# Re-ordering the start, the second batch's loads and scores, the folds and the tail of a fused attention-plus-FFN kernel

## The chip, the cores and the metric

The kernel runs on one core of a Trainium2 chip. The metric is the device time of one execution in microseconds (us), as the median of several. A run counts as slow when it is over 1.5% above the fastest of the same kernel; the texts below compare fast runs unless they say otherwise. "Same" means within 2%.

TensorE does the matmuls (PE in the profile), VectorE is DVE, ScalarE is ACT, GpSimd is POOL and SyncE is SP. Idle time of TensorE is what costs, since it is busy nearly throughout. "Before" is the kernel before the change, "the change" the changed kernel.

## The reference, cut to what matters

```python
# q, k, v: (4, 5824, 256) float32; tau = 1
qn = q / (norm(q, axis=1) + 1e-6);  kn = k / (norm(k, axis=1) + 1e-6)
s  = kn.transpose(0, 2, 1) @ qn / tau          # 256 x 256 for each batch
a  = softmax(s, axis=-1)
x  = (v @ a).reshape(4 * 5824, 256)
out = ((x @ w1) * (x @ w2)) @ w3 @ w_out       # d_ff = 1024
```

The kernel folds the attention matrix into the weights: for each batch, `Wf = a @ (w1, w2)`, so that `v` is multiplied straight by `Wf`; and `W = w3 @ w_out` once. A batch is 11 chunks of 512 tokens and a short one, each with 8 units: two TensorE products a and b of `v` with a part of `Wf`, and their elementwise product. Of the 192 tokens of a short chunk, the 64 beyond 128 are the left-over rows; those of two batches are handled together. The fold needs the whole scores of its batch, and those need all of its q and k.

## The kernel before

All loads come from GpSimd, which casts float32 to bf16 on the way; SyncE issues most transposes of v and most output stores. A batch's q and k come in six pieces each; q has five buffers, k six, v three.

```python
IN_BUFS = {"q": 5, "k": 6, "v": 3}
...
def load_part(nm, n, pi, lo, hi):
    nc.gpsimd.dma_start(
        out=pieces[nm, n, pi][:, lo:hi, :], in_=qk_main[nm, n][0][:, pi * PIECE + lo : pi * PIECE + hi, :]
    )
...
def transpose_piece(n, pi):                     # v is wanted transposed
    ...
        nc.sync.dma_start_transpose(vT[:, pi * PIECE : (pi + 1) * PIECE, :, :], t[:, :, :])
```

Work other than the units is kept in an agenda. Its times are not times of the chip but a sum of the estimated TensorE costs of what has been emitted, the `clock`; I call its unit a clock-us. A unit adds 0.87, a deferred fold 0.43. What is due is emitted between units.

```python
def run_due(upto=None):
    lim = clock[0] if upto is None else upto
    while agenda and agenda[0][0] <= lim:
        _, _, cost, fn = agenda.pop(0)
        clock[0] += cost
        fn()
...
def make_agenda(b):
    clock[0] = 0.0
    if b == 0:
        for i in range(2):
            at(1.5 + 0.6 * i, 0.43, soft0[5 + i])          # two folds left over
        ...
        moves = [("v", 0, 3, 29.0), ("qk", 1, 0, 38.0), ("qk", 1, 1, 43.0), ("v", 0, 4, 50.0), ("qk", 1, 2, 58.0)]
        moves += [("qk", 1, 3, 63.0), ("v", 0, 5, 70.0), ("qk", 1, 4, 81.0), ("qk", 1, 5, 87.0)]
        ...
        t0, t1 = 57.0, 115.5                               # scores of the second batch
```

GpSimd takes the moves in order. Ahead of each, it copies one element of the newest product (a gate: not before TensorE has got there), and, if the move before was a v, one element of that v's **transposed** tile. I call that a hold: the next load isn't issued until the transpose has landed.

```python
for nm, m, pi, t in moves:
    if before is not None:
        at(t, 0.0, lambda w=before: hold(vTs[w[0]][...]))  # nc.gpsimd.tensor_copy(gate_t, src)
    at(t, 0.0, gate)
    if nm == "qk":
        at(t, 0.0, lambda m=m, pi=pi: load_qk(m, pi))
        before = None
    else:
        at(t, 0.0, lambda m=m, pi=pi: load_piece("v", m, pi))
        at(t + 4.0, 0.0, lambda m=m, pi=pi: transpose_piece(m, pi))
        before = (m, pi)
for i, (cst, fn) in enumerate(score_units(n)):
    at(t0 + (t1 - t0) * i / len(units), cst, fn)
```

Of the kernel before, what the change touches and what calls it, by code (L numbers as in the profile page):

```python
# [10 lines left out]
AF = mybir.ActivationFunctionType  # L11
ALU = mybir.AluOpType
F32 = DT.float32
BF16 = DT.bfloat16

P = 128
PIECE = 8
LAG = 2
IN_BUFS = {"q": 5, "k": 6, "v": 3}
MM_COL = 1.0 / 2400.0  # L20
MM_FIX = 0.0025
# [3 lines left out]
def kernel(  # L25
# [213 lines left out]
    def soft_units(n):  # L239
# [102 lines left out]
        def fold_mm(i, c2, tag="ab", on_act=None):  # L342
            h, rest = divmod(i, 4)
            w, c1 = divmod(rest, 2)
            if c2 == 0:
                st["fold", i] = psum.tile(
                    [P, 512], F32, tag=tag, name=f"fold_{n}_{i}", bufs={"ab": 4, "out": 3}[tag]
                )
            nc.tensor.matmul(  # L349
                st["fold", i], lhsT=st["e"][:, c2, c1 * P : (c1 + 1) * P], rhs=w12[:, c2, w, h * 512 : (h + 1) * 512],  # L350
                start=(c2 == 0), stop=(c2 == CT - 1),
            )
            if c2 == CT - 1:
                dst = Wf[n][:, c1, w, h * 512 : (h + 1) * 512]
                if on_act if on_act is not None else i % 2 == 0:
                    nc.scalar.activation(out=dst, in_=st["fold", i], func=AF.Copy, scale=st["rs"][:, c1 : c1 + 1])  # L356
                else:
                    nc.vector.tensor_scalar_mul(dst, st["fold", i], st["rs"][:, c1 : c1 + 1])

        def fold(i, tag="ab", on_act=None):  # L360
            fold_mm(i, 0, tag)
            fold_mm(i, 1, tag, i % 2 == 0 if on_act is None else on_act)

        def first_folds():
            sum_mm(0)
            fold_mm(0, 0)
            fold_mm(1, 0)
            sum_mm(1)
            fold_mm(0, 1)
            fold_mm(1, 1)  # L370
            fold(2)
            transpose_half_on_pe(0, 0, 0, False)
            fold(3, on_act=True)
            fold(4, "out", on_act=False)
            fold(5, "out")

        if n == 0:
            return [k_first, k_row, q_first, scaled_first, first_folds] + [lambda i=i: fold(i) for i in range(6, 8)]
# [7 lines left out]
            + [(0.2, 15.5, sums)]  # L386
            + [(0.43, 16.5 + 0.85 * i, lambda i=i: fold(i)) for i in range(8)]
# [75 lines left out]
    def emit_out(b, c, j, ab):  # L463
# [13 lines left out]
        for s, lhsT in enumerate(lhs):  # L477
            h, o = (s, 0) if small else divmod(s, 2)
            nc.tensor.matmul(  # L479
                tl[h][:, o, :], lhsT=lhsT, rhs=W_sb[:, j, :],  # L480
                start=(j == 0 and o == 0), stop=(j == FT - 1 and (small or o == 1)),
                skip_group_check=True,
            )
        clock[0] += len(lhs) * (D * MM_COL + MM_FIX)
        if j == FT - 1:
            o = work.tile([P, 4, D], F32, tag="o_sb", name=f"osb_{b}_{c}", bufs=3)
            rows = out[b * N : b * N + NT * P, :].rearrange("(p i) c -> p i c", i=NT)
            if small:
                nc.scalar.copy(o[:, 0, :], tl[0][:, 0, :])
                other = nc.scalar if b == B - 1 else nc.sync  # L490
                other.dma_start(out=rows[:, NT - 1, :], in_=o[:, 0, :])
                if b % 2 == 1:
                    o2 = work.tile([P, D], F32, tag="kr", name=f"oleft_{b}", bufs=1)
                    nc.vector.tensor_copy(o2, tl[1][:, 0, :])
                    for k, eng in enumerate((nc.sync, other)):
                        m = b - 1 + k
                        eng.dma_start(out=out[m * N + NT * P : (m + 1) * N, :], in_=o2[k * LEFT : (k + 1) * LEFT, :])
# [4 lines left out]
            del out_tiles[b, c]  # L502
# [9 lines left out]
    busy(14)  # L512
    load_piece("k", 0, 0, (half,))
    load_piece("q", 0, 0, (half,))
# [14 lines left out]
    nc.vector.tensor_tensor_scan(idx, ones_pp, ones_pp, 0.0, ALU.mult, ALU.add)  # L529
    turned = psum.tile([P, 512], F32, tag="ab", name="turned", bufs=4)  # L530
# [31 lines left out]
    for h in range(2):  # L562
        hs = slice(h * F // 2, (h + 1) * F // 2)
        nc.gpsimd.dma_start(out=w12[:, :, 0, hs], in_=w1r[:, :, hs])
        nc.gpsimd.dma_start(out=w12[:, :, 1, hs], in_=w2r[:, :, hs])
        if h == 0:
            new_piece("v", 0, 0)
        load_part("v", 0, 0, h * half, (h + 1) * half)
# [20 lines left out]
    busy(4)  # L589
# [23 lines left out]
    def make_agenda(b):  # L613
# [3 lines left out]
        if b == 0:  # L617
            for i in range(2):
                at(1.5 + 0.6 * i, 0.43, soft0[5 + i])
# [8 lines left out]
            moves = [("v", 0, 3, 29.0), ("qk", 1, 0, 38.0), ("qk", 1, 1, 43.0), ("v", 0, 4, 50.0), ("qk", 1, 2, 58.0)]  # L628
            moves += [("qk", 1, 3, 63.0), ("v", 0, 5, 70.0), ("qk", 1, 4, 81.0), ("qk", 1, 5, 87.0)]
            moves += [("v", 1, 0, 96.0), ("v", 1, 1, 106.0), ("v", 1, 2, 116.0), ("qk", 2, 0, 126.0)]  # L630
            t0, t1 = 57.0, 115.5
        else:
# [4 lines left out]
            t0, t1 = 16.0, 104.0  # L637
# [24 lines left out]
    for b in range(B):  # L662
        make_agenda(b)
        for c in range(NCH):
            for j in range(FT):
# [3 lines left out]
                while w_ready[0] and len(pend) > LAG and npop < 2:  # L669
                    emit_out(*pend.pop(0))  # L670
                    npop += 1
                    run_due()
        run_due(1e9)
    while pend:
        emit_out(*pend.pop(0))
# [35 lines left out]
```

## Time and profile before

| | before |
|---|---|
| median of 3 runs | 573.14 us |
| span of the profiled execution | 571.7 us |
| TensorE busy | 559.4 us |
| first unit starts | 40.7 us |
| last matmul ends | about 567.9 us |

Read the busy row first. TensorE is busy for 98% of the span. Timeline columns are the start in us, the duration, the engine, the line, the operation, and in brackets the idle time before it with what ended it.

```profile
139.19 0.60 PE L188 MATMUL G<-k,q 128*128 128x256 bf16 x4
```

### The profile page before, as it was taken

The page shows a single profiled execution, that of the slowest core. Times are in us where ns is not written, and L with a number is a line of the kernel's source. Part 1 is how long each engine was busy: PE and PEld are TensorE (multiplying, and loading weights), DVE is VectorE, ACT ScalarE, POOL GpSimd, SP SyncE. Part 2 cuts the span into 40 slices and gives each one's busy share as a digit, 9 for nine tenths or more (in the row PEclk, how much of TensorE's full clock was granted, in tenths as well). Part 3 has the DMA queues.
Part 4 walks back from the last instruction along what each step waited for, and adds up shares of the span by engine and source line. Part 5 has one row for each costly group of instructions (what it writes and reads, how often), then busy time and mean ns, then how long its engine had stood idle before and what let it go on. Part 6 is the DMA issues. An engine that isn't in the chain of part 4 may idle for free.

```text
span 571.7 us, 10102 instructions
## 1 busy us (share of the span) xinstructions
PE 559.4 (98%) x3750; PEld 354.5 (62%) x3750; DVE 377.4 (66%) x612; ACT 337.7 (59%) x624; POOL 83.3 (15%) x164
## 2 busy tenths in 40 slices
PE   7789999999999999999999999999999999999997
PEld 4655576776666666666666666666665666666665
DVE  1047744788977567887776667778876656565564
ACT  0046644777856567776766567767766554454453
POOL 5250020303030111121030012031120000000000
PEclk9999999999999999999999999999999999999999
DMA  8999959869685697495661595665640325221011
GB/s 163 211 187 208 184 104 240 170 149 242 140 183 118 123 204 150 94 192 121 145 144 72 99 215 123 140 136 126 175 110 38 85 73 148 63 63 75 38 72 58
DMA packets 74560, 76.93 MB, mean 135 GB/s; under 512 B 54160, under 2 KB 58256, under 8 KB 74512
## 3 DMA queue, kind: packets, MB, share of 16 engines
q0 software_dynamic: 15504, 39.46, 39.3%
q1 hardware_dynamic: 58784, 36.64, 22.2%
q8 instruction: 29, 0.48, 0.3%
q10 hardware_dynamic: 224, 0.20, 0.1%
q14 instruction: 19, 0.16, 0.1%
HBM read 78.91 MB, written 23.86 MB: 180 GB/s over the span
## 4 chain that ended last, share of the span: by engine, by line
PE 92%; DMA 5%; DVE 1%; ACT 1%; POOL 1%; issue 0%; ACTq 0%; POOLq 0%
PE o L479 28%; PE a L438 27%; PE b L438 27%; PE G L188 5%; DMA k<-in_k_dram 5%; PE fold L349 2%; PE w L596 1%; ACT as L444 0%; ACT kr L279 0%; POOL k L109 0%; POOL q L109 0%; DVE abs L453 0%; PE sqk L221 0%; DVE vT L136 0%; DVE abs L455 0%
## 5 line engine op out<-in xcount | busy, mean ns | idle before, releaser
L453 DVE TENSOR_TENSOR abs<-as,b 128x512 bf16<-128x512 bf16 x336 | 230.5, 687 | 141.4 <-ACT as L444 130.3
L444 ACT CAST as<-a 128x512 bf16<-128x512 f32 (+1 forms) x384 | 216.1, 563 | 176.9 <-DVE abs L453 90.2
L438 PEld LDWEIGHTS <-Wf 128*128 128x128 bf16 x1536 | 149.2, 98 | 102.0 <-issue 1.9
L479 PE MATMUL o<-W_sb,abs 128*128 128x256 bf16 x1376 | 209.6, 273 | 0.1
L438 PE MATMUL a<-vT,Wf 128*128 128x512 bf16 x704 | 209.4, 379 | 0.2
L438 PE MATMUL b<-vT,Wf 128*128 128x512 bf16 x704 | 209.3, 379 | 0.0
L479 PEld LDWEIGHTS <-abs 128*128 128x128 bf16 x1376 | 134.5, 98 | 81.6 <-DVE abs L455 0.3
L197 DVE TENSOR_TENSOR acc<-acc,sq 128x1024 f32<-128x1024 f32 x66 | 80.4, 1219 | 0.4 <-ACT sq L185 0.3
L188 PE MATMUL G<-k,q 128*128 128x256 bf16 x276 | 49.9, 273 | 0.0
L185 ACT ACTIVATE sq<-q 128x512 f32<-128x512 bf16 x66 | 41.8, 634 | 0.0
L185 ACT ACTIVATE sq<-k 128x512 f32<-128x512 bf16 x66 | 41.6, 630 | 0.0
L426 POOL COPY gate_t<-abs 1x1 bf16<-1x1 bf16 x39 | 13.9, 355 | 167.7 <-DVE abs L453 167.0
L500 DVE COPY osb<-o 128x512 f32<-128x512 f32 x44 | 30.1, 685 | 0.7 <-PE o L479 0.7
L430 POOL COPY gate_t<-vT 1x1 bf16<-1x1 bf16 x17 | 4.4, 258 | 169.3 <-DMA vT<-v 134.0
L188 PEld LDWEIGHTS <-q 128*128 128x128 bf16 x276 | 27.0, 98 | 3.1
L499 ACT COPY osb<-o 128x512 f32<-128x512 f32 x44 | 25.8, 586 | 3.8 <-PE o L479 1.8
L279 ACT ACTIVATE kr<-row 128x256 f32<-128x256 f32 x1 | 0.4, 385 | 31.6 <-PE row L267 31.6
L109 POOL DMA_DIRECT2D q<-in_q_dram x29 | 15.7, 541 | 13.2 <-DMA k<-in_k_dram 6.0
L349 PE MATMUL fold<-w,e 128*128 128x512 bf16 x64 | 17.0, 380 | 0.5 <-DVE vT L136 0.4
L356 ACT ACTIVATE Wf<-fold,rs 128x512 bf16<-128x512 f32 x16 | 10.9, 688 | 8.1 <-PE fold L349 6.4
L244 DVE TENSOR_TENSOR dk<-sqk,ident 128x256 f32<-128x256 f32 x1 | 0.4, 425 | 21.3 <-PE sqk L221 21.3
L109 POOL DMA_DIRECT2D k<-in_k_dram x25 | 13.8, 551 | 3.7 <-DMA k<-in_k_dram 1.9
(89 smaller groups left out, 240.4 us busy)
## 6 DMA issues: line engine op xcount, KB each, us to landing
out_dram<-osb SPq DMA_DIRECT2D x44, 512.0 KB, 3.1
k<-in_k_dram POOLq DMA_DIRECT2D x19, 512.0 KB, 8.5
v<-in_v_dram POOLq DMA_DIRECT2D x19, 512.0 KB, 5.2
q<-in_q_dram POOLq DMA_DIRECT2D x18, 512.0 KB, 6.6
w_wout<-in_moe_w_dram POOLq DMA_DIRECT2D x1, 2048.0 KB, 23.6
k<-in_k_dram POOLq DMA_DIRECT2D x4, 320.0 KB, 9.9
v<-in_v_dram POOLq DMA_DIRECT2D x4, 320.0 KB, 5.4
q<-in_q_dram POOLq DMA_DIRECT2D x4, 256.0 KB, 12.0
```

Of the source, the lines that this page charges most:

```text
L109: nc.gpsimd.dma_start(out=pieces[nm, n, pi][:, lo:hi, :], in_=qk_main[nm, n][0][:, pi * PIECE + lo : pi * PIECE + hi, :])
L185: nc.scalar.activation(out=dst[:, :, part, :], in_=src[:, o : o + 2, :], func=AF.Square)
L188: nc.tensor.matmul(G[:, ct, :], lhsT=qt[:, i, ct * P : (ct + 1) * P], rhs=kt[:, i, :], start=(pr == 0 and part == 0 and ct == 0), stop=(pr ...
L197: nc.vector.tensor_add(accs[n], accs[n], sqs[0])
L349: nc.tensor.matmul(st["fold", i], lhsT=st["e"][:, c2, c1 * P : (c1 + 1) * P], rhs=w12[:, c2, w, h * 512 : (h + 1) * 512], start=(c2 == 0), ...
L426: nc.gpsimd.tensor_copy(gate_t, last_ab[0][:1, :1])
L438: nc.tensor.matmul(t[:, :n], lhsT=Wf[b][:, ct, w, j * P : (j + 1) * P], rhs=rhs_of(b, c, ct), start=(ct == 0), stop=(ct == CT - 1),)
L444: nc.scalar.copy(a_sb[:, :n], tiles[0][:, :n])
L453: nc.vector.tensor_mul(ab, a_sb, tiles[1])
L479: nc.tensor.matmul(tl[h][:, o, :], lhsT=lhsT, rhs=W_sb[:, j, :], start=(j == 0 and o == 0), stop=(j == FT - 1 and (small or o == 1)), skip ...
L499: nc.scalar.copy(o[:, 0:2, :], tl[0])
L500: nc.vector.tensor_copy(o[:, 2:4, :], tl[1])
```

## The change

The intent is to fill idle time of TensorE at the start, at the three batch changes and at the end. (1) The first halves of the first q and k come as float32 from SyncE and are cast on chip. (2) The first batch's folds are done by quarters, so that the first unit can start after one quarter; more folds are left for later. (3) In the first batch, the loads of the second batch's q and k go ahead of late v pieces, and the scores run from 46 to 104 clock-us in place of 57 to 115.5. (4) In later batches scores end sooner, softmax and folds are spaced further out, and every second fold uses the scores' one-buffer bank G of PSUM (TensorE's output memory) in place of the four buffers "ab" of the units. (5) In the last short chunk the outputs are held back by five units, and at the end the left-over rows go first. The cut leaves out the new functions, the order of v's first load among the weights, and one transpose of v that moves ahead of the first fold.

```diff
+LAG_END = 5
...
-            + [(0.2, 15.5, sums)]
-            + [(0.43, 16.5 + 0.85 * i, lambda i=i: fold(i)) for i in range(8)]
+            + [(0.2, 16.5, sums)]
+            + [(0.43, 17.8 + 0.9 * i, lambda i=i: fold(i, "G" if i % 2 else "ab")) for i in range(8)]
...
-    busy(14)
-    load_piece("k", 0, 0, (half,))
-    load_piece("q", 0, 0, (half,))
+    busy(10)
+    raw = {}
+    for nm in "kq":
+        new_piece(nm, 0, 0)
+        raw[nm] = work.tile([P, half, C], F32, tag="o_sb", name=f"raw_{nm}", bufs=3)
+        nc.sync.dma_start(out=raw[nm], in_=qk_main[nm, 0][0][:, :half, :])
+        load_part(nm, 0, 0, half, PIECE)
...
+    nc.vector.tensor_copy(pieces["k", 0, 0][:, :half, :], raw["k"])
+    nc.scalar.copy(pieces["q", 0, 0][:, :half, :], raw["q"])
...
-    for h in range(2):
-        hs = slice(h * F // 2, (h + 1) * F // 2)
...
+    for f0, f1 in ((0, 256), (256, 512), (512, F)):
+        nc.gpsimd.dma_start(out=w12[:, :, 0, f0:f1], in_=w1r[:, :, f0:f1])
+        nc.gpsimd.dma_start(out=w12[:, :, 1, f0:f1], in_=w2r[:, :, f0:f1])
...
-            for i in range(2):
-                at(1.5 + 0.6 * i, 0.43, soft0[5 + i])
+            at(0.5, 0.87, soft0[5])
+            for i in range(4):
+                at(2.3 + 0.6 * i, 0.43, soft0[6 + i])
...
-            moves = [("v", 0, 3, 29.0), ("qk", 1, 0, 38.0), ("qk", 1, 1, 43.0), ("v", 0, 4, 50.0), ("qk", 1, 2, 58.0)]
-            moves += [("qk", 1, 3, 63.0), ("v", 0, 5, 70.0), ("qk", 1, 4, 81.0), ("qk", 1, 5, 87.0)]
-            moves += [("v", 1, 0, 96.0), ("v", 1, 1, 106.0), ("v", 1, 2, 116.0), ("qk", 2, 0, 126.0)]
-            t0, t1 = 57.0, 115.5
+            moves = [("qk", 1, 0, 29.0), ("v", 0, 3, 30.0), ("qk", 1, 1, 43.0), ("qk", 1, 2, 47.0), ("v", 0, 4, 53.0)]
+            moves += [("qk", 1, 3, 62.0), ("qk", 1, 4, 66.0), ("v", 0, 5, 72.0), ("qk", 1, 5, 81.0)]
+            moves += [("v", 1, 0, 94.0), ("v", 1, 1, 104.0), ("v", 1, 2, 114.0), ("qk", 2, 0, 126.0)]
+            t0, t1 = 46.0, 104.0
...
-            t0, t1 = 16.0, 104.0
+            t0, t1 = 16.0, 99.0
...
-                while w_ready[0] and len(pend) > LAG and npop < 2:
+                lag = LAG_END if b == B - 1 and c == NCH - 1 else LAG
+                while w_ready[0] and len(pend) > lag and npop < 2:
...
-    while pend:
-        emit_out(*pend.pop(0))
+    for only in (1, 0):
+        for p in pend:
+            emit_out(*p, only=only)
```

More of the change, by code (lines that the diff above doesn't have):

```diff
@@ L340, in sums, with fold_mm @@
             sum_mm(1)
-        def fold_mm(i, c2, tag="ab", on_act=None):
-            h, rest = divmod(i, 4)
-            w, c1 = divmod(rest, 2)
+        def fold_mm(key, c2, tag="ab", on_act=True):
+            w, c1, lo, hi = key
             if c2 == 0:
-                st["fold", i] = psum.tile(
-                    [P, 512], F32, tag=tag, name=f"fold_{n}_{i}", bufs={"ab": 4, "out": 3}[tag]
+                st[key] = psum.tile(
+                    [P, 512], F32, tag=tag, name=f"fold_{n}_{w}_{c1}_{lo}", bufs={"ab": 4, "out": 3, "G": 1}[tag]
                 )
+            m = st[key][:, : hi - lo]
             nc.tensor.matmul(
-                st["fold", i], lhsT=st["e"][:, c2, c1 * P : (c1 + 1) * P], rhs=w12[:, c2, w, h * 512 : (h + 1) * 512],
+                m, lhsT=st["e"][:, c2, c1 * P : (c1 + 1) * P], rhs=w12[:, c2, w, lo:hi],
                 start=(c2 == 0), stop=(c2 == CT - 1),
@@ L353, in fold_mm @@
             if c2 == CT - 1:
-                dst = Wf[n][:, c1, w, h * 512 : (h + 1) * 512]
-                if on_act if on_act is not None else i % 2 == 0:
-                    nc.scalar.activation(out=dst, in_=st["fold", i], func=AF.Copy, scale=st["rs"][:, c1 : c1 + 1])
-                else:
-                    nc.vector.tensor_scalar_mul(dst, st["fold", i], st["rs"][:, c1 : c1 + 1])
-        def fold(i, tag="ab", on_act=None):
-            fold_mm(i, 0, tag)
-            fold_mm(i, 1, tag, i % 2 == 0 if on_act is None else on_act)
+                dst = Wf[n][:, c1, w, lo:hi]
@@ new lines, in fold_mm, with fold, quarter_mm @@
+                if on_act:
+                    nc.scalar.activation(out=dst, in_=m, func=AF.Copy, scale=st["rs"][:, c1 : c1 + 1])
+                else:
+                    nc.vector.tensor_scalar_mul(dst, m, st["rs"][:, c1 : c1 + 1])
+        def fold(i, tag="ab"):
+            h, rest = divmod(i, 4)
+            w, c1 = divmod(rest, 2)
+            for c2 in range(CT):
+                fold_mm((w, c1, h * 512, (h + 1) * 512), c2, tag, i % 2 == 0)
+        def quarter_mm(lo, c1, c2):
+            if c2 == 0:
+                tag = "ab" if lo == 0 else "out"
+                st[lo, c1] = psum.tile(
+                    [P, 2, 256], F32, tag=tag, name=f"quarter_{lo}_{c1}", bufs={"ab": 4, "out": 3}[tag]
+                )
+            m = st[lo, c1]
+            for w in range(2):
+                nc.tensor.matmul(
+                    m[:, w, :], lhsT=st["e"][:, c2, c1 * P : (c1 + 1) * P], rhs=w12[:, c2, w, lo : lo + 256],
+                    start=(c2 == 0 and w == 0), stop=(c2 == CT - 1 and w == 1), skip_group_check=True,
+                )
+            if c2 == CT - 1:
+                for o in (0, P) if lo == 0 else (slice(0, 256),):
+                    cols = slice(o, o + P) if lo == 0 else o
+                    dst, src = Wf[n][:, c1, :, lo : lo + 256][:, :, cols], m[:, :, cols]
+                    if c1 == 0:
+                        nc.scalar.activation(out=dst, in_=src, func=AF.Copy, scale=st["rs"][:, c1 : c1 + 1])
+                    else:
+                        nc.vector.tensor_scalar_mul(dst, src, st["rs"][:, c1 : c1 + 1])
@@ L364, in first_folds @@
         def first_folds():
             sum_mm(0)
-            fold_mm(0, 0)
-            fold_mm(1, 0)
+            for c1 in range(CT):
+                quarter_mm(0, c1, 0)
             sum_mm(1)
-            fold_mm(0, 1)
-            fold_mm(1, 1)
-            fold(2)
-            transpose_half_on_pe(0, 0, 0, False)
-            fold(3, on_act=True)
-            fold(4, "out", on_act=False)
-            fold(5, "out")
+            for c1 in range(CT):
+                quarter_mm(0, c1, 1)
@@ L377, in soft_units, with second_quarter @@
+        def second_quarter():
+            for c1 in range(CT):
+                for c2 in range(CT):
+                    quarter_mm(256, c1, c2)
         if n == 0:
-            return [k_first, k_row, q_first, scaled_first, first_folds] + [lambda i=i: fold(i) for i in range(6, 8)]
+            return [k_first, k_row, q_first, scaled_first, first_folds, second_quarter] + [lambda i=i: fold(i) for i in range(4, 8)]
         return (
@@ L461, in emit_ab, with emit_out @@
         clock[0] += 4 * (n * MM_COL + MM_FIX)
-    def emit_out(b, c, j, ab):
+    def emit_out(b, c, j, ab, only=None):
         small = c == NCH - 1
@@ L477, in emit_out @@
         for s, lhsT in enumerate(lhs):
+            if only is not None and s != only:
+                continue
             h, o = (s, 0) if small else divmod(s, 2)
@@ L483, in emit_out @@
             )
-        clock[0] += len(lhs) * (D * MM_COL + MM_FIX)
+        clock[0] += (len(lhs) if only is None else 1) * (D * MM_COL + MM_FIX)
         if j == FT - 1:
@@ L488, in emit_out @@
             if small:
-                nc.scalar.copy(o[:, 0, :], tl[0][:, 0, :])
                 other = nc.scalar if b == B - 1 else nc.sync
-                other.dma_start(out=rows[:, NT - 1, :], in_=o[:, 0, :])
-                if b % 2 == 1:
+                if only != 1:
+                    nc.scalar.copy(o[:, 0, :], tl[0][:, 0, :])
+                    other.dma_start(out=rows[:, NT - 1, :], in_=o[:, 0, :])
+                if b % 2 == 1 and only != 0:
                     o2 = work.tile([P, D], F32, tag="kr", name=f"oleft_{b}", bufs=1)
@@ L501, in emit_out @@
                 nc.sync.dma_start(out=rows[:, 4 * c : 4 * c + 4, :], in_=o)
-            del out_tiles[b, c]
+            if only is None:
+                del out_tiles[b, c]
     NDEF = 4
@@ L561 @@
     load_piece("q", 0, 5, (1, 3, 4))
-    for h in range(2):
-        hs = slice(h * F // 2, (h + 1) * F // 2)
-        nc.gpsimd.dma_start(out=w12[:, :, 0, hs], in_=w1r[:, :, hs])
-        nc.gpsimd.dma_start(out=w12[:, :, 1, hs], in_=w2r[:, :, hs])
-        if h == 0:
-            new_piece("v", 0, 0)
-        load_part("v", 0, 0, h * half, (h + 1) * half)
+    new_piece("v", 0, 0)
+    load_part("v", 0, 0, 0, half)
+    for f0, f1 in ((0, 256), (256, 512), (512, F)):
+        nc.gpsimd.dma_start(out=w12[:, :, 0, f0:f1], in_=w1r[:, :, f0:f1])
+        nc.gpsimd.dma_start(out=w12[:, :, 1, f0:f1], in_=w2r[:, :, f0:f1])
+    load_part("v", 0, 0, half, PIECE)
     load_piece("v", 0, 1)
@@ L588 @@
     soft0[3]()
-    busy(4)
+    busy(3)
+    transpose_half_on_pe(0, 0, 0, False)
     soft0[4]()
```

## The prediction

> **What bounds the kernel now.** I read the page first, then the busy time by stretches, then the timeline of the two ends. The page:
>
> ```profile
> PE 559.4 (98%) x3750; PEld 354.5 (62%) x3750; DVE 377.4 (66%) x612; ACT 337.7 (59%) x624; POOL 83.3 (15%) x164
> ...
> PE   7789999999999999999999999999999999999997
> ```
>
> TensorE is the bound: 559.4 of 571.7 us, and its row of slices is short of 9 only in the first three and the last. So 12.3 us of idle time is all that a re-ordering can win (plus warm-up matmuls, which count as busy). Where it lies, by stretches (first column the stretch, then its length, then PE busy; the last two are the DMA share and GB/s, bf16 side):
>
> ```profile
> 0.00:5.90 5.90, 4.66 (x14) 1.68 (x14) 0.94 (x6) 1.28 (x1) 4.87 (x13) 1.00 0.58 91
> 5.90:34.70 28.80, 23.95 (x289) 20.31 (x289) 1.43 (x6) 1.01 (x3) 10.49 (x19) 1.00 1.10 205
> 34.70:40.70 6.00, 4.40 (x31) 1.99 (x30) 3.75 (x13) 3.88 (x9) 2.79 (x5) 1.00 1.16 182
> 40.70:562.00 521.30, 520.62 (x3368) 325.75 (x3367) 366.54 (x570) 328.16 (x602) 65.13 (x129) 1.00 0.60 132
> 562.00:572.00 10.00, 5.71 (x56) 4.74 (x54) 4.75 (x19) 3.41 (x10) 0.00 (x0) 0.95 0.22 79
> ```
>
> Idle: 1.24 + 4.85 + 1.60 in the start, 0.68 in the whole middle, the rest (4.3) at the end, of which some 3.8 lies after the last matmul (567.86). The middle runs without gaps: only the start, three batch changes and the tail are left to win. The start's stretch 5.9 to 34.7 is bound by the load of the first q and k: PE waits at each piece, DMA share is 1.1. The chain in order of time shows this and what follows:
>
> ```profile
> 1.22 0.69 POOL k L109
> ...
> 4.52 11.89 DMA k<-in_k_dram
> 16.41 0.28 issue
> 16.69 14.79 DMA k<-in_k_dram
> 31.48 0.05 issue
> 31.53 0.84 PE sqk L221 x12
> ...
> 36.46 0.52 ACT e L318
> ...
> 39.82 1.04 PE fold L349 x4
> 40.85 0.22 PE a L438
> ```
>
> The last k lands at 31.5; then norms and softmax; e exists at 36.98; six folds of 0.43 us; the first a at 40.69.
>
> **What the Trainium skill says.** (1) "DMA: Bandwidth & Descriptors", Specifications: first byte about 1 us after issue from GpSimd, about 0.6 us from SyncE. The trace agrees with the first: GpSimd's first load is issued at 1.22, and by one-microsecond stretches nothing moves before 2.0, 27 GB/s in 2 to 3, 125 in 3 to 4 and 203 from 4 on. No load of before is issued from SyncE, so the second is untested. (2) The same page, "Issuing engines are not separate DMA queues": queues interleave on the same 16 engines, several issuers save only issuing time. So the SyncE load can bring forward the start of the stream, not its rate of about 210 GB/s. (3) "TensorE: Matmul & The Clock Gate", Part 1: about 3.4 us of activity lift the half clock. The trace: warm-up matmuls are 0.43 us apart up to 4.55, five more then by 5.9. Ten in place of fourteen still pass that point.
>
> **The change part by part.**
>
> *First q and k by SyncE, as float32, cast on chip.* SyncE is free at 0.7 us, GpSimd issues at 1.22 and needs 0.54 us for each. Before, by 4.0 us the stream has moved (27+125) GB/s x 1 us = 0.15 MB, so at 208 GB/s it runs 3.3 us behind a stream that was full from zero. With SyncE's issue at about 0.75 and 0.6 to 1 us to the first byte it would be 1.7 to 2.2 us behind. Gain 1.1 to 1.6; I take 1.3. float32 arrives in the same bytes read, so I expect no dearer transfer. The two casts (1024 elements, one on DVE, one on ACT) are hidden: those engines are idle then, and PE waits for k piece 1 until 11.58 anyway. As the stretch to 31.5 is DMA-bound, this shifts everything behind it: **-1.3**.
>
> *Quarters folded first.* I took the built order of the queues and walked PE, ACT and DVE through it with the trace's durations (ab pair 0.87, ACT copy 0.59, DVE product 0.69, fold 0.43, its eviction 0.69 ACT or 0.75 DVE, vT copy 0.69 DVE, about 0.2 from matmul to reader, 0.07 overlap of neighbours). In before's clock: the transposes of v move into the softmax gap (v's first half is now ahead of the weights, about 34.6, slack 1.9). rs exists at 38.15; the first quarter's evictions take 0.40, so the first a starts at 38.6 in place of 40.69, 2.1 us sooner. But 2.60 us of folds (0.87 + 4 x 0.43) are left for later against 0.87 before: 1.73 of the 2.1 is only postponed. What is left, 0.4, has to pay for a new wait: the last fold (second half, w2, c1=1) is emitted behind a v transpose right before unit j=4, which needs it. DVE's queue from 43.2 is product, fold, product, vT copy, fold: 0.69+0.75+0.69+0.69+0.75 with a gap of 0.3, ending about 46.8, while PE wants it at 45.7. Stall 1.06. The same walk over before gives the observed first a (40.70) and ends unit 23 at 63.95 (the trace: about 63.65); over after it ends at 64.61. So **+0.65**. Folds that start with other folds unfinished win nothing by themselves on a PE that is busy anyway.
>
> *q and k ahead of late v, scores 46 to 104 in place of 57 to 115.5, softmax and folds with the G bank.* Work is moved, none removed. The middle loses 0.68 us in all; the visible gaps are at the three batch changes (0.14 in 175:180, 0.13 in 300:320, 0.41 in 430:450), where folds and the short chunk compete for ACT and DVE. Folds that are done before the short chunk can remove about 0.4: **-0.4**. DVE's load with scores beside the catch-up (one product and two outs per 1.74 us) is the regime of before's 100:130, 24.55 of 30 us with PE full, so no new stall.
>
> *Outs held back by five, left rows first.* Before:
>
> ```profile
> 567.45 0.28 PE L479 MATMUL o<-W_sb,abs 128*128 128x256 bf16 x1
> 567.58 0.28 PE L479 MATMUL o<-W_sb,left 128*128 128x256 bf16 x1
> ...
> 567.77 0.37 ACT L489 COPY osb<-o 128x256 f32<-128x256 f32 x1 [0.70 <-PE o L479]
> 568.17 0.38 ACTq L491 DMA_DIRECT2D out_dram<-osb  x1
> 568.60 0.53 ACTq L497 DMA_DIRECT2D out_dram<-oleft  x1
> ```
>
> Three units' outs (3 x 0.22 = 0.66) move behind the last product, where PE waited 0.33. But the first three short units then run without outs: PE needs 0.34 per unit, DVE 0.45 (0.29+0.21 less overlap), so about 0.4 is lost there. After the last unit: four lefts (0.44), a wait for the last left product, one left, five main rows (0.55). ACT issues the left rows' DMA in its own queue ahead of the main copy: that waits for DVE's copy (0.42) and takes 0.53, then copy 0.37, issue 0.38, landing 1.7. From the end of the last b: before 1.92 to the last issue + 2.0 to landing = 3.9; after 2.17 + 0.40 + 1.7 = 4.3, less 0.66, plus 0.4: 4.0. **+0.1**.
>
> Sum: -1.3 + 0.65 - 0.4 + 0.1 = -0.95, so 572.2. My walk is slightly pessimistic (0.3 on before), and more of the 0.6 us of the SyncE path may be won: I say **571.8**.
>
> **Rivals.** (a) *The quarters win outright*, 1 to 2 us, and the total is 570: for it, the first a is 2 us sooner; against, the postponed folds and the saturated DVE between 43 and 47. It needs DVE to be quicker than its durations. (b) *The small weight loads are late*: rows of 256 columns are half as long; at 30 to 34 us the rate already falls to 135 to 193 GB/s with row-wise weights and small pieces. If the first quarter of w2 lands after 37.0 (before's clock), the first a waits; or v piece 1 comes after its transposes, which PE now wants about 1 us nearer to its landing (44.7). That gives back 0.5 to 1.5: 573. (c) *The SyncE stream starts no sooner or splits the engines badly*, and PE's order waits for the casts: then -1.3 is nearer to -0.3: 572.8. (d) *Nothing at the ends counts because the middle bounds it*: excluded, the ends are in series with the middle.
>
> **Range and chances.** The terms err by about 0.5 (load), 0.7 (quarters), 0.3 (batch changes), 0.4 (tail), together about 1.0, so eight in ten is about 1.5 to each side: 570.2 to 573.2. Two per cent is 11.5 us, nearly all of the idle time: same is nearly certain.
>
> **What would show it.** Load: last k landing near 30.2 and q/k bytes moving before 2 us. Quarters: first a near 37.3, and a PE wait of about 1 us on DVE's fold eviction near 45.5, inside the fifth unit. Middle: idle under 0.4 between units. Tail: ACT's copy behind its own DMA issue, and short waits of PE on DVE in the short chunk. Wrong if DMA's first bytes don't come earlier, if that DVE stall is absent (then 570.5), or if PE gets gaps while scores run beside the catch-up (then over 573).

## More of the kernel before

```profile
92.19 0.53 POOL L109 DMA_DIRECT2D v<-in_v_dram  x1 [0.27 <-issue]
105.42 0.60 POOL L430 COPY gate_t<-vT 1x1 bf16<-1x1 bf16 x1 [12.71 <-DMA vT<-v]
...
128.65 0.54 POOL L109 DMA_DIRECT2D k<-in_k_dram  x1
```

The second line is a hold: GpSimd sits for 12.71 us until the transpose of v has landed. The third line is the load of the fifth k piece of the second batch. It took 10.2 us to land (the view of DMA issues), so it was there at 128.65 + 10.2 = 138.85; the line at 139.19 has the matmuls that want it.

## The result, and the profile after

The changed kernel took 579.86 us (median of 6, 577.91 to 580.36); the kernel before took 573.24 us beside it (6 runs, 572.98 to 575.30). The ratio is 1.0103 [1.0083, 1.0124]: "same" at 2%, but slower by 1% where I had predicted 0.2% faster, and far outside my range. Ratios here are the mean time of one kernel's fast runs over that of the other's of the same rounds, with a 95% interval in brackets, so not quite the ratio of the medians. The profiled run took 578.99 us with a span of 576.9, against 573.43 and 571.7.

The page of the changed kernel: the busy row, and two rows in 40 slices of 14.4 us (tenths busy; granted clock in tenths).

```profile
PE 560.3 (97%) x3746; PEld 355.5 (62%) x3753; DVE 379.0 (66%) x614; ACT 338.9 (59%) x626; POOL 85.5 (15%) x164
PE   8889999989999999999999999999999999999997
PEclk9999999989999999999999999999999999999999
```

The first four slices are better than before (8889 against 7789), but the ninth slice, 115 to 130 us, falls to 8 in both rows. Nothing of the kind is in the page of before. The busy time by stretches (stretch, length, then busy us of PE, PEld, DVE, ACT, POOL, then granted clock, DMA share, GB/s) narrows it down:

```profile
0.00:37.65 37.65, 30.44 (x318) 23.13 (x321) 5.97 (x26) 5.76 (x12) 18.51 (x35) 1.00 1.06 203
37.65:46.00 8.35, 7.42 (x43) 3.91 (x45) 5.80 (x9) 5.11 (x9) 0.30 (x1) 1.00 1.14 207
46.00:114.00 68.00, 68.00 (x459) 44.04 (x458) 46.64 (x64) 42.83 (x77) 10.64 (x23) 1.00 0.91 187
114.00:119.00 5.00, 2.07 (x13) 1.30 (x12) 1.82 (x2) 1.22 (x2) 1.19 (x3) 0.93 1.07 214
119.00:125.00 6.00, 6.00 (x36) 3.81 (x35) 3.60 (x5) 3.87 (x7) 0.00 (x0) 0.78 0.94 182
```

From 46 to 114 TensorE has no gap at all. In the five microseconds after 114 it is busy for 2.07, and then it is busy all the time but at a granted clock of 0.78: 36 matmul records in 6 us, where before had 46 in the same stretch. TensorE's timeline names what it waited for (five of its lines):

```profile
37.67 0.60 PE L464 MATMUL a<-vT,Wf 128*128 128x512 bf16 x2 [0.56 <-DVE Wf L388]
45.84 0.39 PE L464 MATMUL b<-vT,Wf 128*128 128x512 bf16 x1 [0.85 <-DVE Wf L360]
114.63 0.60 PE L508 MATMUL o<-W_sb,abs 128*128 128x256 bf16 x4
118.16 0.53 PE L189 MATMUL G<-k,q 128*128 128x256 bf16 x2 [2.93 <-DMA k<-in_k_dram]
175.54 0.59 PE L351 MATMUL fold<-w,e 128*128 128x512 bf16 x2 [0.47 <-DVE Wf L360]
```

The fourth line is the loss: the fourth k piece of the second batch landed at 118.1 and was wanted at 115.2. The second line is the predicted stall on DVE's fold; the fifth is a new one, at the batch change. GpSimd's timeline shows why the k piece was late (four of its lines; L110 issues loads, L456 is the hold):

```profile
93.95 0.53 POOL L110 DMA_DIRECT2D v<-in_v_dram  x1
109.33 0.18 POOL L456 COPY gate_t<-vT 1x1 bf16<-1x1 bf16 x1 [14.85 <-DMA vT<-v]
110.68 0.53 POOL L110 DMA_DIRECT2D q<-in_q_dram  x1
111.20 0.54 POOL L110 DMA_DIRECT2D k<-in_k_dram  x1
```

v is issued at 93.95 and takes 11.5 us; its transpose is issued by SyncE at 105.52 and lands 3.7 us later; the hold ends at 109.33; the gate and the issues bring k to 111.20; k takes 6.9 us: 118.1. The DMA view of 93 to 112 us shows in 40 slices of 0.475 us how busy the DMA engines were while this chain ran:

```profile
DMA  9999999999999999999998100000099999989917
```

The six zeros (103.9 to 106.8) are the time between v's data and its transpose: the DMA share there is 0.02. This idle stretch comes from the order of the steps, and it is about as long as the gap. Around it the engines were full (share 1.00 from 94.0 to 103.9, 1.01 from 106.8 to 112), so the length of the loads themselves counts too. How much of the lateness belongs to the serial order and how much to the loads, this trace doesn't settle.

The tail came as predicted: the left rows' DMA issue sits in ACT's own queue ahead of the main copy.

```profile
573.21 0.56 ACTq L527 DMA_DIRECT2D out_dram<-oleft  x1
573.87 0.37 ACT L520 COPY osb<-o 128x256 f32<-128x256 f32 x1 [1.95 <-PE o L508]
574.27 0.35 ACTq L521 DMA_DIRECT2D out_dram<-osb  x1
```

**Where the time came from.** The last matmuls of the last unit of the second batch start at 319.89 in place of 314.50, 5.39 us later. (At the end of the first batch, 186.71 and 180.48, the two can't be compared: before still has three folds to do there.) Found up to there: the gap 2.93; the low clock 1.67 (one minus the granted clock, times busy time, summed over half-microseconds from 118 to 122); waits for folds at the two batch changes 0.47 + 0.47, less the 0.14 + 0.13 of before, 0.67; less 0.24 that the start gained net. That is 5.03; 0.36 is not assigned. The profiled run is 0.9 below the median of the six, which one trace can't explain.

### The profile page after: what moved, and what is told of

Its sections match the earlier page's. It is cut to its first block, busy times and chain, and to the rows that moved or that the text cites. A ratio compares the mean times of both kernels' runs of the same rounds, so it can differ in the third digit from the quotient of the medians.

```text
span 576.9 us, 10120 instructions
## 1 busy us (share of the span) xinstructions
PE 560.3 (97%) x3746; PEld 355.5 (62%) x3753; DVE 379.0 (66%) x614; ACT 338.9 (59%) x626; POOL 85.5 (15%) x164
## 4 chain that ended last, share of the span: by engine, by line
PE 86%; ACT 2%; DMA 2%; DVE 2%; issue 1%; ACTq 0%; POOL 0%; POOLq 0%
PE o L508 26%; PE b L464 26%; PE a L464 26%; PE G L189 5%; PE fold L351 1%; PE w L633 1%; DMA k<-in_k_dram 1%; ACT as L470 1%; DVE abs L479 1%; DMA out_dram<-osb 1%; DVE Wf L360 0%; DVE s L314 0%; ACT Wf L358 0%; ACT e L319 0%; ACT kr L280 0%
## 5 line engine op out<-in xcount | busy, mean ns | idle before, releaser
L452 POOL COPY gate_t<-abs 1x1 bf16<-1x1 bf16 x39 | 18.5, 475 | 177.4 <-DVE abs L479 176.9
L456 POOL COPY gate_t<-vT 1x1 bf16<-1x1 bf16 x17 | 3.0, 177 | 174.9 <-DMA vT<-v 165.7
L110 POOL DMA_DIRECT2D q<-in_q_dram x28 | 15.1, 540 | 12.3 <-DMA k<-in_k_dram 5.1
L351 PE MATMUL fold<-w,e 128*128 128x512 bf16 x52 | 14.0, 379 | 1.6 <-DVE Wf L360 1.4
L479 DVE TENSOR_TENSOR abq<-as,b 128x512 bf16<-128x512 bf16 x16 | 10.9, 686 | 5.4 <-ACT as L470 4.8
L358 ACT ACTIVATE Wf<-fold,rs 128x512 bf16<-128x512 f32 x14 | 9.6, 688 | 8.2 <-PE fold L351 6.8
L110 POOL DMA_DIRECT2D k<-in_k_dram x24 | 13.5, 564 | 4.3 <-DMA k<-in_k_dram 3.5
```

The lines of the kernel that those rows point to most:

```text
L110: nc.gpsimd.dma_start(out=pieces[nm, n, pi][:, lo:hi, :], in_=qk_main[nm, n][0][:, pi * PIECE + lo : pi * PIECE + hi, :])
L351: nc.tensor.matmul(m, lhsT=st["e"][:, c2, c1 * P : (c1 + 1) * P], rhs=w12[:, c2, w, lo:hi], start=(c2 == 0), stop=(c2 == CT - 1),)
L452: nc.gpsimd.tensor_copy(gate_t, last_ab[0][:1, :1])
L479: nc.vector.tensor_mul(ab, a_sb, tiles[1])
```

## The experiments

All 18 kernels gave correct results. Each was run against the kernel before on the same chip. "Piece" means a q and k piece of the second batch, counted from one.

Run 1 is e1 in the table, and so on.

| run | what | median, us | ratio to before [95%] |
|---|---|---|---|
| e1 | change, with old b=0 order and times | 577.18 | 1.0064 [1.0049, 1.0080] |
| e2 | change, old score times alone | 574.76 | 1.0023 [1.0007, 1.0040] |
| e3 | change, old load order alone | 597.88 | 1.0429 [1.0410, 1.0448] |
| e4 | change, warm-up matmuls in the gap | 578.42 | 1.0083 [1.0067, 1.0099] |
| e5 | before + new b=0 order and times | 576.20 | 1.0041 [1.0026, 1.0057] |
| e6 | before + SyncE start | 572.65 | 0.9983 [0.9971, 0.9996] |
| e7 | before + G-bank folds, later softmax | 574.67 | 1.0022 [1.0010, 1.0035] |
| e8 | before + new tail | 573.84 | 1.0001 [0.9988, 1.0015] |
| e9 | before + quarters | 578.26 | 1.0086 [1.0071, 1.0101] |
| e10 | e2, ab-bank folds, one fold sooner | 572.99 | 0.9993 [0.9981, 1.0005] |
| e11 | change, fourth piece ahead of v | 578.85 | 1.0096 [1.0078, 1.0115] |
| e12 | e11, ab-bank folds, fold sooner, old tail | 576.08 | 1.0051 [1.0039, 1.0063] |
| e13 | change without holds | 598.09 | 1.0404 [1.0365, 1.0443] |
| e14 | quarters, scores 3 later | 574.12 | 1.0019 [1.0005, 1.0032] |
| e15 | SyncE start, scores 2 later | 572.51 | 0.9991 [0.9979, 1.0004] |
| e16 | SyncE start, no holds, old order | 572.34 | 0.9984 [0.9971, 0.9996] |
| e17 | e16 + quarters + fold sooner | 573.05 | 1.0017 [0.9977, 1.0057] |
| e18 | e17, scores 1.7 later | 590.49, mostly slow | 1.0007 [0.9984, 1.0030] on two fast runs |

**The theory** was that scores 11 clock-us sooner outrun the load chain, and that this gap and the low clock behind it are the loss. **The rivals**: the load order itself is at fault; the quarters or the fold bank are; the start's faster work collides with something.

### Runs 1 to 3: order and times apart

```diff
 # e1: both lines below; e2: the second alone; e3: the first alone (in after)
-moves = [("qk", 1, 0, 29.0), ("v", 0, 3, 30.0), ...]      # new order
+moves = [("v", 0, 3, 29.0), ("qk", 1, 0, 38.0), ...]      # old order
-t0, t1 = 46.0, 104.0
+t0, t1 = 57.0, 115.5
```

> The changed kernel with the first batch's load order and its score times (57 to 115.5) put back as before; all else stays changed. Theory A (the loss is the TensorE gap of 2.9 us at 115 us, where the fourth piece of the next k lands late, plus the half clock that follows, some 2 us, together about 5): about 574.5 (573.5 to 575.5), no idle of TensorE over 0.6 us between 50 and 170 us. Rival B (the loss is in the folds with one G bank, 3 x 0.47, the fold wait of 0.85 at 45 us and the tail): 577 or more.

> The changed kernel with only the first batch's score times put back (57 to 115.5), the new load order kept. Theory A says that the fourth piece lands at about 118 us and is first wanted 11 us later than now, so no gap: about 574.5, like the run with both put back. If the new load order by itself loses time (contention of loads, transposes and writes), it stays above 576.5.

> The changed kernel with only the first batch's load order put back, the new earlier score times (46 to 104) kept. Theory A says that each piece has its deadline 11 us earlier while the third piece is issued at about 106.6 us (as before) and lands at about 113, where it is wanted at about 104: a longer gap, 6 to 9 us, and a cold clock after it: 582 to 588. If the new order was the cause and not the deadline, about 574.5.

Run 2 came out as expected: with the scores at the old times the wait for k is gone, and with it 0.8% of the 1.03%. Run 3 shows that the order is not at fault: old order with the new times is much worse (waits for k of 15.8 us in all, the longest 6.5; I had expected 582 to 588). The **new order makes the new times cheaper**, but it isn't enough.

Run 1 was a miss, 577.18 against an expected 574.5. The trace has a wait for k of 1.39 us at 138.18, at the fifth piece. That is the piece whose slack in the kernel before is 0.34 us. In run 1 only the start and the first batch's folds differ before that point, and together they bring the fifth piece's matmuls forward by more than this slack. So there are two ways to a late piece: moving the scores, and moving everything.

### Run 4: how much is the low clock

```diff
 for i, (cst, fn) in enumerate(units):
+    if b == 0 and i == 36:
+        at(t0 + (t1 - t0) * i / len(units), 0.0, lambda: busy(13))
     at(t0 + (t1 - t0) * i / len(units), cst, fn)
```

> The changed kernel with 13 warm-up matmuls (13 x 0.217 = 2.8 us) ahead of the score matmul that waits at 115 us. They fill the gap with work that is worth nothing. If the half clock after the gap costs by itself, it goes away: 1.5 to 2.0 us faster than the changed kernel (about 578), granted clock 1.00 from 110 to 130 us. If the gap alone is the loss, the time stays within 0.5 us of the changed kernel (579.4 to 580.4).

Thirteen matmuls without use fill the gap. The granted clock then stays at 1.00, the wait for k shrinks to 0.4 us, and the ratio falls from 1.0103 to 1.0083, 0.0020 of 573 or about 1.15 us. The two ratios come from different rounds and their intervals overlap, so the times alone don't show it. The traces do: the last unit of the second batch starts at 318.49 in place of 319.89, 1.40 us sooner. The trace of the change puts the low clock at 1.67, and the matmuls and the rest of the wait (13 x 0.217 + 0.45 = 3.27) take 0.34 more than the gap: 1.33. So the low clock is a cost beside the gap, and smaller than it.

### Runs 5 to 9: each part alone on the kernel before

```diff
 # e5: the b=0 moves and t0, t1 of the change      # e6: raw_k, raw_q from SyncE and two casts, busy(10)
 # e7: fold(i, "G" if i % 2 else "ab"), 16.5, 17.8 + 0.9 * i, t1 = 99.0
 # e8: LAG_END = 5 and the split last loop         # e9: quarter_mm, weights in three parts, five deferred folds
```

> The kernel before with only the first batch's new load order and earlier score times (46 to 104). Theory A (deadlines ahead of the held loads): a gap of 2 to 3.5 us at the fourth piece and a cold clock after it, 576.5 to 579. If the loss needs the quicker start of the changed kernel too, 573 to 575.

> The kernel before with only the first q and k by SyncE and the casts. The load of the first q and k ends 1.0 to 1.3 us sooner (last k near 30.3). If nothing takes it back, 572.2. But the fifth piece of the second batch's k lands about 1 us before it is wanted in the kernel before, so I expect part of it to come back as a wait there: 572.3 to 573.2, with a wait of TensorE on k of 0 to 0.8 us near 138 us.

> The kernel before with only the folds of batches 1 to 3 in turn in the G bank, later softmax offsets and scores of batches 1 and 2 ending at 99. The walk of the changed kernel's waits says 0.47 to 0.97 us of TensorE wait on VectorE's fold eviction at each batch change, 1.5 to 2.0 in all, against 0.68 before: 573.9 to 574.8. The rival, that the G bank frees the ab banks and so the gaps go, says 572.8.

> The kernel before with only the last outs held back by five, left rows first. My sum for the tail says +0.1 (0.66 moved, 0.4 lost in the short chunk, ACT's copy behind its own DMA issue): 573.2 to 573.8. If the held outs fill the last wait for free: 572.7.

> The kernel before with only the quarters folded first (with the order of the weight loads, the transposes of v in the softmax gap and the smaller filler). The walk of the queues in the prediction said +0.65; the changed kernel's profile shows a 0.85 us wait of the fifth unit on VectorE's fold eviction and 0.56 us before the first a. 573.5 to 574.6, unless the late k piece near 140 us adds a wait. If quarters win outright (first a 2 us sooner kept): below 572.5.

Run 5 has the loss with nothing else of the change in it: a wait for k of 2.89 us at 119.52 and 1.53 us of low clock, 576.20 (a little less than expected). The new order and times are sufficient for the gap. The time of the profiled run rose by only 3.05 us, though gap and low clock add up to 4.42; 0.57 of the rest is a first unit that started sooner (40.12 against 40.69), which this edit doesn't explain.

Run 6 is the one part that paid: -0.17%, about 1.0 us, and the wait of 0.33 us on the fifth piece that it was expected to run into. Its last wait for the first k ended at 30.65, 0.9 us sooner than before; 1.0 to 1.3 was expected.

Run 7: the waits of TensorE between 160 and 460 us, which covers the three batch changes (what waited, for what; us in total, times, longest):

```profile
PE fold L349 <- DVE Wf L358: 2.1, 5, 0.5
```

Every second fold uses the one-buffer bank G, and the next of them must wait until DVE has read the last. These are 2.1 us, where the visible idle of before at the three changes is 0.68. As expected, this part costs (+0.22%), and my prediction had it down as a gain. Run 10 keeps the later offsets and score ends and puts only the bank back: there these waits are gone, so they belong to the bank.

Run 8: the tail is worth nothing, as expected. Its profiled run, 577.66, was the longest of its runs, and holds a surprise, since the code is that of before up to the last chunk:

```profile
141.81 1.01 PE L189 MATMUL G<-k,q 128*128 128x256 bf16 x4 [2.83 <-DMA k<-in_k_dram]
```

So this wait comes in some executions without any change ahead of it. Here k was issued at 129.15 and took 12.6 us to land, where before it was issued at 128.65 and took 10.2; the slack was only 0.34 us. A few runs of before lie at 574.55 to 577.62 too; they were not profiled, so that it is the same cause is not shown.

Run 9 was a clear miss: 578.26 where 573.5 to 574.6 was expected.

```profile
140.41 0.38 PE L189 MATMUL G<-k,q 128*128 128x256 bf16 x2 [2.91 <-DMA k<-in_k_dram]
```

The same wait again, at the fifth piece. The quarters leave 0.87 + 4 x 0.43 = 2.59 clock-us of folds for the agenda, where before leaves 2 x 0.43 = 0.86. The clock counts them, so everything due by it (loads and scores) comes with 1.73 us less of unit work done. A move that seems to concern the first 10 us shifts the deadlines at 140: TensorE wanted the fifth piece at 137.50, in before at 139.19. Less the slack of 0.34 that is 1.35 of the wait. The rest is a later landing (140.4 against 138.85: issued 0.7 later and 11.0 us under way in place of 10.2), whose cause is not shown. In this profile the clock stayed at 1.00 through a gap of 2.91 us.

### Run 10: taking the losses out

```diff
 # e2, and:
-fold(i, "G" if i % 2 else "ab")
+fold(i)
-at(4.0, 0.5, lambda: transpose_half_on_pe(0, 0, 1, False))
+at(4.2, 0.5, lambda: transpose_half_on_pe(0, 0, 1, False))   # the last deferred fold now goes first
```

> The changed kernel with the old score times of the first batch (run 2 measured 574.8), all folds of batches 1 to 3 in the ab banks, and the last fold of the first batch ahead of the v transpose. If the G bank costs about 1.2 us and the fold behind the transpose 0.6: 573.0 (572.4 to 573.6), no wait of TensorE on a fold eviction over 0.3 us. If the G bank only moved the waits: 574.5.

A hit at 572.99. In its trace the fold waits are gone and 0.18 us is left at 45.37 where the change has 0.85. With the score times, the fold bank and one fold's place put right, the 1.03% is gone: the three causes together account for the loss (0.9993, interval 0.9981 to 1.0005).

### Runs 11 and 12: mending the order

```diff
-("qk", 1, 2, 47.0), ("v", 0, 4, 53.0)] ... [("qk", 1, 3, 62.0), ...
+("qk", 1, 2, 47.0), ("qk", 1, 3, 52.0)] ... [("v", 0, 4, 55.0), ...
 # e12 also: fold(i), the 4.2 of e10, the old tail
```

> The changed kernel with one move: the fourth q and k pieces are issued ahead of the v piece whose transpose now holds them back. If the hold is what makes them late, they land near 105 us and the gap at 115 us is gone; the fifth piece is then held by that v piece and lands at 122 to 125, wanted at about 124, so a short wait may appear there: 575 to 577.5. If plain DMA throughput makes the piece late, the gap moves to an earlier or later piece at full size and the time stays at 579 to 580.

> All mends together: fourth q and k piece ahead of the held v piece, folds of batches 1 to 3 in the ab banks, last fold of the first batch ahead of the v transpose, tail as before; SyncE start, quarters and early scores kept. If the fifth piece is in time: 572.2 to 573.2, at or under the kernel before. If it waits as the fourth did: 574 to 576.

The mend failed. With the fourth piece ahead of the held v, its gap is gone, but the second piece is late by 0.6 (96.7 us) and the sixth by 2.3 (138.68). Run 12 has gaps of 1.1 and 2.4 (576.08, just over the 574 to 576 that I had given for a fifth piece that waits). A new order only picks which piece comes late: run 11 waits for k for 2.9 us in all, as much as the change, and took 578.85. That is nearer to what I had written for "plain DMA throughput" (the gap moves at full size, 579 to 580) than to what I had written for the hold (575 to 577.5). So scores from 46 to 104 ask for the pieces faster than they come; whether the holds or the DMA engines set that pace, these two runs leave open.

### Run 13: without the holds

```diff
-if before is not None:
+if before is not None and not (nm == "qk" and m == 1 and pi > 0):
```

> The changed kernel without the copies that hold the second batch's q and k pieces until a v transpose has landed (the gates on the progress of the units stay, and all data waits). If the hold makes the pieces late: the fourth piece is issued near 101 in place of 110.7 us, lands before 110, no wait of TensorE on k, 574.5 to 576 (the folds' waits, about 2.3 us, stay). If throughput makes them late: a wait of 2 us or more stays somewhere, 578 to 580.

If the hold makes the chain serial, taking it out of the way of pieces two to six should bring them sooner. (It only paces the queues: without it the kernel has no race, and its results were correct.) I expected 574.5 to 576, or 578 to 580 if throughput makes them late. It took 598.09, in fast runs all, so neither came true. SyncE's timeline, the landing times of its transpose, the stretch 102 to 114, and TensorE's longest wait:

```profile
83.66 17.37 SPq L156 DMA_TRANSPOSE vT<-v  x1
```

```profile
DMA to landing us min/median/max: 43.0/43.0/43.0
```

```profile
102.00:114.00 12.00, 6.89 (x39) 4.30 (x38) 4.95 (x6) 3.71 (x7) 3.10 (x5) 0.76 1.34 43
```

```profile
130.64 0.59 PE L508 MATMUL o<-W_sb,abs 128*128 128x256 bf16 x2 [14.43 <-ACT osb L529]
```

The transpose ran beside GpSimd's casting loads and took 17.37 us to be issued and 43.0 to land; in the kernel before such a transpose lands in 3.6 to 5.1 (median 4.1). The DMA engines counted as full (share 1.34) while moving 43 GB/s, against 187 in the stretch from 46 to 114 us of the change. Outputs are stored from SyncE too, behind that transpose, so the output buffers ran out, and TensorE waited 14.43 us for ACT to get one. It also waited 5.11 us for k (at 110.30). In this order the holds are needed: without them transposes and casting loads run side by side. That it is this meeting which makes the transpose slow is inferred from the trace; run 16 shows that it doesn't always.

### Runs 14 and 15: the deadline alone

```diff
 # e14: e9 with                 # e15: e6 with
-t0, t1 = 57.0, 115.5
+t0, t1 = 60.0, 118.5           # 59.0, 117.5 in e15
```

> Quarters alone (run 9: 578.3) with the first batch's scores 3 us later on the schedule (60 to 118.5). If run 9's loss is the late fifth piece: no wait on k, 573.4 to 574.6, that is +0.3 to +1.2 over before for the quarters themselves. If it is the quarters' own cost, it stays above 576.

> SyncE start alone (run 6: 572.65 with a 0.33 us wait on k) with scores 2 us later on the schedule. Wait on k gone: 572.2 to 572.6. If the later softmax costs at the batch change what the wait cost: 572.6 to 573.2.

Run 14 is the test of run 9's reading: the same quarters with the scores 3 clock-us later take 574.12 in place of 578.26. So most of run 9's loss was the late piece. The profile, of the slowest of the four, still has a wait of 1.41 at 142.87; what the quarters cost by themselves is about 1 us (0.19%) or less. Run 15 has no wait for k, but its interval overlaps that of run 6: no gain is shown.

### Runs 16 to 18: a better kernel

```diff
 # e16: e6 with the condition of e13
 # e17: e9, with e6's start, e13's condition and e10's 4.2
 # e18: e17 with t0, t1 = 58.7, 117.2
```

> SyncE start alone without the holds ahead of the second batch's q and k pieces. No wait on k, pieces earlier by some us: 572.0 to 572.5. If loads beside the transposes slow the transposes or the writes, a new wait on vT or on an output buffer shows and it is 573 or more.

> The kernel before with the SyncE start, the quarters, the last fold ahead of the v transpose, and no holds ahead of the second batch's q and k (old load order, old score times, old folds and tail). If the parts add: 572.34 (run 16) less 0 to 0.4: 571.9 to 572.4. If the quarters, which put the schedule's clock 1.7 us ahead of the work, bring the late piece or a transpose beside loads back: a wait of TensorE on k or vT near 105 to 145 us and 574 or more.

> The same with the scores 1.7 us later on the schedule (58.7 to 117.2), which takes back what the quarters put the clock ahead. No wait on k: 571.8 to 572.5, and if run 17 shows a wait, this one is faster by its size.

Run 16 has the lowest median of all, 572.34, with no wait for k; its ratio is that of run 6 (0.9984 and 0.9983), so what its missing holds are worth can't be told. Under the old order the transposes took 3.6 to 9.3 us without holds. What the trace does show is the fifth k piece:

```profile
121.98 0.54 POOL L109 DMA_DIRECT2D k<-in_k_dram  x1
```

It took 9.1 us to land, so it was there at 131.1; in run 6, with the holds, it was issued at 129.06 and landed at 138.6. In this order the hold did make the piece late. Run 16 is a little faster than the kernel before (0.16%, the interval ends at 0.9996) and clearly faster than the change.

Run 17 was a miss: 573.05 with one run at 580.44, where 571.9 to 572.4 was expected. Its profile shows a transpose of 16.8 us to landing and a wait of 1.9 us for an output buffer: the same pair as in run 13, smaller. Run 18 stays **undecided**: four of its six runs are slow (587.88 to 596.54), the two fast ones are 572.52 and 575.13. The profile is of one of the slow ones (595.95), so it is not compared with the others. It shows the pair of runs 13 and 17 once more, a transpose that landed after 35.0 us and a wait of 21.1 us of TensorE for an output buffer, most of the 23.4 us that separate this run from the fastest. The other three slow ones were not profiled, so their cause is not shown.

## Why the prediction was wrong

**The bound: right.** TensorE had no idle time to spare in the middle, and that is why a gap of 2.93 us was paid in full, and more.

**The SyncE load, -1.3: right in its mechanism, smaller in the total.** The last k of the first batch was expected at 30.2 and the last wait for it ended at 30.26 (31.53 before). Bytes moved from 1.6 us on. But a new wait of 0.41 for q follows at 31.62, and when the scores end the lead is 0.8 (33.93 against 34.74). Alone it gave -0.17%, about 1.0 us.

**The quarters, +0.65: right in what it named, blind to what it did later.** The first unit came at 37.67 (37.3 predicted) and DVE's fold stalled the fifth unit for 0.85 us at 45.84 (1.06 near 45.5; with the gap of 0.3 that its sum names, the queue from 43.2 would end at 47.07 and not at 46.8, so the 1.06 leaves the gap out). Load and quarters together were to gain 0.65 and gained 0.24: the sum for the change came out right, partly by luck since the lead in it shrank (unit 23 ends at 64.61 - 1.3 = 63.31, measured 63.37), the walk over before was 0.3 late. I took that 0.3 as a reason to go lower; it was one to go higher. I had also written that 1.73 us of the gain is "only postponed". I did not ask what else is timed by the clock that counts the postponed folds. It moved all later deadlines by those 1.73 us (run 9, and run 14 against it).

**The scores: here the prediction failed.** The step reads "*q and k ahead of late v, scores 46 to 104 in place of 57 to 115.5, softmax and folds with the G bank.* Work is moved, none removed", and ends in "-0.4" and "so no new stall". For the stall I looked at DVE's load (rightly: from 46 to 114 TensorE waits for nothing) and never at when the pieces land. What failed is the overlap of scores and loads: the step took for granted that the q and k pieces would be there when the earlier scores ask for them. The numbers were in the trace of before. Its fourth piece lands near 120.9 and is wanted at 129.2, 8.3 us of slack. In the change it is wanted at 115.2, 14.0 us sooner (11 from the agenda, the rest from the start and the order of units), and the new order brings it only 2.8 us sooner (118.1), because it is the piece behind the held v: 8.3 + 2.8 - 14.0 = -2.9, which is the gap. Measured: a gap of 2.93 and 1.67 of low clock (run 2 takes them away; run 5 has them alone; run 3 shows that the times and not the new order are the cause).

**The folds in bank G, inside the same -0.4: the wrong sign.** They cost 0.22% alone, about 1.3 us, by waits of 0.5 us on a bank with one buffer (run 7); in the change, 0.47 at each of the three batch changes.

**The tail, +0.1: right as far as it can be seen.** 0.01% alone, with an interval of about 0.8 us to each side (run 8). In the traces, from the last unit of the third batch (447.82 before, 452.96 in the change) to the end of the span it is 123.9 us in both. ACT's copy comes behind its own DMA issue as described.

**The rivals and the range.** None of the four rivals was this. The last sentence named it ("if PE gets gaps while scores run beside the catch-up (then over 573)") but put no chance on it, so the range had no room for it. Its width came from the errors of terms I had, not from one that I lacked.

What stays open: 0.36 us of the 5.39 in the trace, the 0.9 us between the profiled run and the median, run 18, and, in the change's own order, how much of the pieces' lateness is the holds and how much the DMA engines' load: run 16 shows the hold for the fifth piece of the old order, run 11 looks like throughput, and run 13 was spoiled by the slow transpose.

## What to carry to other kernels

Before work is moved to an earlier time, list for each transfer that it needs when it lands and when it is wanted in the trace at hand: a wait of zero can mean 8 us of slack or 0.34. Where one schedule clock times everything, any step that charges it moves all later deadlines. A wait that looks idle may be what keeps two kinds of transfer apart, so test its removal alone before building on it.

## What the Trainium skill lacked or had wrong

- "DMA: Bandwidth & Descriptors", Rules for kernel authors: it says that a transpose next to ordinary DMAs needs nothing. That holds for the results (all 18 runs were correct), but the page lacks the price: beside GpSimd's casting loads a transpose took 43.0 us to land (run 13) and 16.8 (run 17), against 3.6 to 5.1 in the kernel before, while in run 13 the DMA engines counted as full moved 43 GB/s. Run 16 (3.6 to 9.3 us) shows that it doesn't always come to that; what decides it, and whether it is the loads that do it, these runs don't show.
- "TensorE: Matmul & The Clock Gate", Part 1: its table of the two states gives at least one idle window of about 3.4 us for the fall to the half clock, and its text calls the window free-running. Here gaps of 2.93 us (the change), 2.89 (run 5) and 2.83 (run 8) were already followed by 1.4 to 1.7 us lost to a lower granted clock, and one of 2.36 (run 12) by a clock of 0.50 from 140 to 143 us; gaps of 2.91 (run 9) and 2.27 (run 11) were not. So the fall came without a gap of that length, and the length of the gap alone doesn't decide it; what does, these runs don't show.
- The same DMA page, Specifications: about 0.6 us to the first byte from SyncE; it lacks from where this is counted. Here SyncE's first load instruction ran from 0.73 to 1.13 us, and nothing moved before 1.6 (82 GB/s from 1.6 to 1.8): 0.9 us or a little more from its start, 0.5 to 0.7 from its end.
